# How the last output-projection loads are cut in a fused attention and gated-MLP decode kernel

## The chip, the cores and the metric

The kernel runs on one core of one Trainium2 chip. The metric is the device time of one execution in microseconds, as the median of several runs; the profile is of one further execution, and its span runs from the first to the last recorded instruction.

## The reference

One token `x` (576 values) is normalised and goes through two branches, whose results are added to `x`.

```python
xn = _layernorm(x)
# A: attention over the last W = 4096 keys, 32 query heads on 16 key/value heads of 128
q = (xn @ wq)                       # 576 -> 4096
p = softmax(q k^T * 128 ** -0.5)
o = p v                             # 32 heads x 128 = 4096 values
a = o @ wo                          # 4096 -> 576
# B: gated MLP, 576 -> 2 x 2304 -> 576
z = gelu(xn @ w_in)
b = (z[:2304] * (w_sp * layernorm(z[2304:]) + b_sp)) @ w_out
out = x + a + b
```

All is bf16. The weights and the needed part of the caches come to 51 MB, each byte of which is read once.

## The kernel before

Almost all of the time goes into reading. One engine's queue (SP's) issues every large load, in an order written out by hand, into four large slots of SBUF, tagged `a` to `d`: `wq`, then groups of four heads of K and V (`load_kv`), `w_in` between them, and at the end `w_out` and `wo`. A slot is loaded again as soon as its last reader is done. Each load is one DMA that runs on all 16 DMA engines; on each of these the loads of the queue follow one another. Five small loads (three pieces of `x`, two scalars) come from ScalarE's queue.

The order of work on the other engines is also the order of the program (`manual_schedule`). For each of four groups of heads, VectorE transposes K (`keys`, L264), TensorE makes scores (`scores`, L271), `sm_a` and `sm_b` make the softmax and put the probabilities in place, `pv` multiplies with V (L335), and `tail` normalises (L345, L349), selects (L356) and writes a quarter of the column tile `Y` (`y_copy`, L363). The `w_in` product and the gate lie between the groups and leave their result in `hv`.

The output projection is at the end. `wo` has 4096 rows; they are read as 128 partitions with 32 rows each, so that "row block" t is row t of every partition, 1152 bytes a partition. `Y[:, t, 1]` is the column that belongs to block t. `w_out` has 18 such blocks (`NF`). A block needs four matmuls with two-wide weights (`out_mms`, L471): the 576 columns are cut in four quarters of 144 (`QW`), and two accumulators in PSUM, `acc[0]` and `acc[1]`, take two quarters each, one in each of two rows: the middle column of three holds the values and the other two zeros, so that the choice of `1 - r:3 - r` picks the row. TensorE runs in order: `out_hv` (w_out) around `tail(3)`, then the 32 blocks of wo as they come, then the two copies into `res` (L486, L487) and the store (L488).

The blocks of wo come in five loads (L108, issued at L82), of 14, 9, 6, 2 and 1 blocks. The first two go to the slot of tag `d` (`ends[1]`), the others behind `w_out` in that of tag `a` (`ends[0]`).

The tile framework gives the loads of all queues eight DMA semaphores in turn, in the order of the program as it runs them, and lets a load wait until the load that had its semaphore before has landed. K's second group, whose slot is free from the start, so has a wait for the first piece of `x`.

## Time and profile before

| | |
|---|---|
| median of 3 runs | 126.90 us (126.83 to 126.94) |
| the profiled execution | 126.97 us, span 125.1 us |
| mean granted TensorE clock | 0.754 |
| HBM read | 50.96 MB, 407 GB/s over the span |
| share of the 16 DMA engines' time, SP's queue | 95.3% |
| TensorE matmul busy | 70.2 us (56%) |
| VectorE busy | 78.6 us (63%) |
| ScalarE busy | 43.2 us (34%) |
| GpSimd busy | 7.2 us (6%) |

Times on the page and in the trace count from the start of the span; 1.9 us of the execution lie outside it. A line of the timeline or of a group gives the source line, the engine, the operation and `out<-in` with the tiles' names; the bracket gives idle time of the engine just before and what ended it. `SPq` is SP's sequencer, which issues loads. In the chain of waits, "DMA end<-in_A_wo_dram" is the time from the issue of a wo load to its landing.

### The profile page before, as it was taken

Reading aid. Unit: us, or ns where it says so; the run is one execution under the profiler, and the core shown is the slowest. Engines: PE = TensorE matmul, PEld = TensorE weight load, DVE = VectorE, ACT = ScalarE, POOL = GpSimd, SP = SyncE. Lnnn points to the kernel's source line nnn. Section 1 sums busy time; section 2 is a strip of 40 time slices with the busy share of each in tenths; the row PEclk is TensorE's granted clock in tenths of the full one; section 3 lists DMA queues with packets and bytes.
Section 4 is the critical chain, followed back from the end, with each engine's and each line's share of the span. In section 5 each row is a group of like instructions: output and inputs, shape, how many; then the busy total and the mean of one; then the engine's idle time right before and its main releaser. Section 6 shows DMA issues by size and latency. Waiting matters only on the chain.

```text
span 125.1 us, 1826 instructions
## 1 busy us (share of the span) xinstructions
PE 70.2 (56%) x728; PEld 30.4 (24%) x728; DVE 78.6 (63%) x152; ACT 43.2 (34%) x101; POOL 7.2 (6%) x21
## 2 busy tenths in 40 slices
PE   0012841009886659999580991059892931059972
PEld 0011201001101002999100031002212311026961
DVE  6845135899699976509999367999938359003200
ACT  2100011000000974998079009608701941940000
POOL 2972000000000000000000000000000100000000
PEclk9999997555599958655568599558997555555999
DMA  4999899998999999898999989899998989999960
GB/s 113 507 422 440 363 503 409 430 482 356 498 389 433 385 482 471 377 492 341 492 430 419 471 367 487 359 482 440 409 482 356 492 374 453 414 434 409 413 248 0
DMA packets 2613, 51.06 MB, mean 408 GB/s; under 512 B 300, under 2 KB 430, under 8 KB 686
## 3 DMA queue, kind: packets, MB, share of 16 engines
q1 hardware_dynamic: 2592, 50.96, 95.3%
q8 instruction: 5, 0.08, 0.2%
q14 instruction: 2, 0.02, 0.0%
q10 hardware_dynamic: 14, 0.00, 0.0%
HBM read 50.96 MB, written 0.00 MB: 407 GB/s over the span
## 4 chain that ended last, share of the span: by engine, by line
DMA 62%; DVE 30%; PE 4%; SPq 1%; issue 1%; ACT 0%; DVEq 0%
DMA k<-in_A_k_cache_dram 36%; DMA end<-in_A_wo_dram 25%; DVE kT L264 22%; DVE pt L309 4%; PE S L271 3%; SPq L82 1%; DVE mx L292 1%; DVE on L349 1%; DVE om L345 1%; PE acc L471 0%; PE yps L356 0%; DVE rs L326 0%; ACT res L487 0%; DVE mt L281 0%; DVE mb L287 0%
## 5 line engine op out<-in xcount | busy, mean ns | idle before, releaser
L271 PE MATMUL S<-kT,Qb 128*8 128x512 bf16 x128 | 32.4, 1145 | 23.2 <-DVE kT L264 22.7
L264 DVE STREAM_TRANSPOSE kT<-k 128x1024 f32<-128x1024 f32 x32 | 36.8, 1207 | 6.2 <-DMA k<-in_A_k_cache_dram 6.2
L298 ACT ACTIVATE pz<-S,nm 32x1024 bf16<-32x1024 f32 x16 | 19.2, 1198 | 34.0 <-DVE nm L295 21.1
L312 ACT COPY PT<-pt 32x128 f32<-32x128 f32 x64 | 19.9, 311 | 16.5 <-DVE pt L309 15.8
L335 PE MATMUL ops<-v,PT 128*32 128x512 bf16 x128 | 11.0, 506 | 6.8 <-ACT PT L312 6.8
L271 PEld LDWEIGHTS <-Qb 128*8 128x8 bf16 x128 | 3.6, 96 | 44.9 <-issue 35.4
L309 DVE STREAM_TRANSPOSE pt<-pz 128x1024 f32<-128x1024 f32 x8 | 9.4, 1210 | 0.8 <-ACT pz L298 0.8
L345 DVE SCALAR_TENSOR_TENSOR om<-ops,rs,dmask 128x512 f32<-128x512 f32 x4 | 3.0, 751 | 10.5 <-PE ops L335 10.3
L371 PEld LDWEIGHTS <-win 128*128 128x128 bf16 x126 | 7.9, 166 | 2.0 <-issue 2.0
L371 PE MATMUL zps<-XT,win 128*128 128x2 bf16 x126 | 8.0, 202 | 0.0
L292 DVE TENSOR_REDUCE mx<-S 128x1 f32<-128x1024 f32 x4 | 4.9, 1216 | 4.0 <-PE S L271 3.9
L335 PEld LDWEIGHTS <-PT 128*32 128x32 bf16 x128 | 3.8, 118 | 11.4 <-ACT PT L312 6.9
L229 ACT CAST q_rep<-qps 128x512 bf16<-128x512 f32 x2 | 1.2, 585 | 14.9 <-DVE q_rep L231 14.9
L410 POOL TENSOR_TENSOR mz<-mz,mhalf 128x1 f32<-128x1 f32 x1 | 0.6, 553 | 84.9 <-DVE mz L409 84.9
L186 PE MATMUL ps_x<-ones_b,xtw 1*128 1x1 bf16 x9 | 0.4, 162 | 8.9 <-DVE xtw L184 8.9
L471 PE MATMUL acc<-end,Y 128*2 128x144 bf16 x128 | 4.5, 226 | 0.9 <-DMA end<-in_A_wo_dram 0.8
L231 DVE CAST q_rep<-qps 128x512 bf16<-128x512 f32 x2 | 1.4, 692 | 4.9 <-PE qps L220 4.2
L487 ACT CAST res<-acc 2x144 bf16<-2x144 f32 x1 | 0.3, 270 | 12.0 <-PE acc L471 12.0
L471 PEld LDWEIGHTS <-Y 128*2 128x2 bf16 x128 | 4.1, 84 | 1.2 <-issue 1.2
L356 PE MATMUL yps<-on,sel 128*32 128x32 f32 x32 | 2.0, 210 | 4.1 <-DVE on L349 4.1
L349 DVE TENSOR_REDUCE on<-om 128x128 f32<-128x512 f32 x4 | 4.2, 1043 | 0.1
L486 DVE CAST res<-acc 2x144 bf16<-2x144 f32 x1 | 0.3, 295 | 5.7 <-PE acc L471 5.7
(96 smaller groups left out, 57.6 us busy)
## 6 DMA issues: line engine op xcount, KB each, us to landing
k<-in_A_k_cache_dram SPq DMA_DIRECT2D x4, 4096.0 KB
v<-in_A_v_cache_dram SPq DMA_DIRECT2D x4, 4096.0 KB, 25.4
win<-in_B_w_in_dram SPq DMA_DIRECT2D x1, 4032.0 KB, 26.9
wq<-in_A_wq_dram SPq DMA_DIRECT2D x1, 3584.0 KB, 12.8
end<-in_B_w_out_dram SPq DMA_DIRECT2D x1, 2592.0 KB, 22.3
end<-in_A_wo_dram SPq DMA_DIRECT2D x1, 2016.0 KB
end<-in_A_wo_dram SPq DMA_DIRECT2D x1, 1296.0 KB
rest<-in_B_w_in_dram SPq DMA_DIRECT2D x1, 1152.0 KB
```

The source lines that it names most:

```text
L264: nc.vector.transpose(dst[:, 1024 * n:1024 * (n + 1)], src[:, 1024 * n:1024 * (n + 1)])
L271: nc.tensor.matmul(S[g % 2][32 * x:32 * x + 8, c, :], lhsT=Qb[:, GK * g + x, be].rearrange("p a h -> p (a h)"), rhs=kv[:, be // 2, be % 2, x],
L292: nc.vector.tensor_reduce(out=mx[:, 0:1], in_=s[:], op=ALU.max, axis=mybir.AxisListType.XY)
L298: nc.scalar.activation(pz[lo:hi, :, :, x, :], s[lo:hi].rearrange("p a (t r e) -> p (a t) r e", r=8, e=2), ACT.Exp, bias=nm[lo:hi, 0:1], sc ...
L309: nc.vector.transpose(dst[:, 1024 * n:1024 * (n + 1)], src[:, 1024 * n:1024 * (n + 1)])
L312: nc.scalar.copy(PT4[32 * a:32 * a + 32, :, x, :], pt[32 * x:32 * x + 32, :, 2 * a:2 * a + 2])
L335: nc.tensor.matmul(ops[32 * q:32 * q + 32, :], lhsT=d["PT"][:, t0 // 2:t0 // 2 + 2].rearrange("p t x h e -> p (t x h e)"), rhs=V[g][:, t0: ...
L345: nc.vector.scalar_tensor_tensor(out=om[:].rearrange("p c d -> p (c d)"), in0=ops[:], scalar=d["rs"][:, 0:1], in1=dmask[:].rearrange("p c ...
L349: nc.vector.reduce_sum(on[:], om[:].rearrange("p c d -> p d c"), axis=AXX)
L356: nc.tensor.matmul(yps[32 * g:32 * g + 32, :], lhsT=sel[:, dq, :], rhs=d["on"][:, 32 * dq:32 * dq + 32], start=(dq == 0), stop=(dq == 3), ...
L371: nc.tensor.matmul(zps[:, :, t], lhsT=wt[:, t, :], rhs=XT[:, s, :], start=(s == 0 and t == 0), stop=(s == NS - 1 and t == NF - 1), skip_gr ...
L471: nc.tensor.matmul(acc[n], lhsT=lhs[:, col, 1 - r:3 - r], rhs=wv[:, QW * (2 * r + n):QW * (2 * r + n + 1)], start=False, stop=(last and r ...
```

## The change

The 32 blocks of wo are cut otherwise. Blocks 0 to 25 come in loads of 14 and 12 blocks into the slot of tag `d`, blocks 26 to 28 in one load behind `w_out`. Of block 31, the last 432 columns (864 bytes a partition) come apart from the rest: 128 rows that go into a tile `ext` of their own, 25 rows a load, alternately to partitions 0 to 24 and 80 to 104, two loads to each of `ext`'s three columns of tiles. The three rows left over (125 to 127) are loaded one by one, early, behind the second K group. Block 30 and the first 144 columns of block 31 follow in one load (1440 bytes a partition, they adjoin in memory), and block 29 is the last. That is ten loads for wo at the end instead of five, and three early ones.

Since rows of block 31 now lie in other partitions than the column `Y[:, 31]`, three matmuls with 0/1 weights (`move`, cut from the identity) move that column, and a copy writes it to `Yx`, with a zero where no row lies. `out_ext(j)` does the three quarters of `ext`'s tile j. Tiles 0 and 1 are done before block 26, tile 2 after block 28, then block 30, the first quarter of block 31, and block 29.

All loads from `w_in` on stand lower in the program's text, behind the constants, in the same order of SP's queue; ahead of them come GpSimd's memset of `ext` and the three 1-row loads, which wait for it.

```diff
+XR = 25
+XB = 80
+XN = 3
...
-    win_sb = rows("a", win_h, "win", 0, 7) + rows(rest, win_h, "win", 7, 2, 4096)
-    K[2] = load_kv("b", A_k_cache, 2, "k")
...
-    wo_sb = []
-    for n, t, at in ((14, 1, 0), (9, 1, 14), (6, 0, NF), (2, 0, NF + 6), (1, 0, NF + 8)):
-        wo_sb += rows(ends[t], A_wo, "wo", len(wo_sb), n, at * D)
...
+    ext = const.tile([P, XN, D - QW], BF16, name="ext")
+    nc.gpsimd.memset(ext[:], 0.0)
+    last = A_wo.rearrange("(p s) c -> p s c", p=P)[:, 31, QW:D]
+    for i in range(P - 5 * XR):
+        nc.sync.dma_start(ext[XB + i:XB + i + 1, 2, :], last[5 * XR + i:5 * XR + i + 1])
+    win_sb = rows("a", win_h, "win", 0, 7) + rows(rest, win_h, "win", 7, 2, 4096)
+    K[2] = load_kv("b", A_k_cache, 2, "k")
...
+    for n, t, at in ((14, 1, 0), (12, 1, 14), (3, 0, NF)):
+        wo_sb += rows(ends[t], A_wo, "wo", len(wo_sb), n, at * D)
+    for j in range(5):
+        lo = XB * (j % 2)
+        nc.sync.dma_start(ext[lo:lo + XR, j // 2, :], last[XR * j:XR * j + XR])
+    wo_p = A_wo.rearrange("(p s) c -> p (s c)", p=P)
+    at, w30 = (NF + 3) * D, D + QW
+    nc.sync.dma_start(ends[0][:, at:at + w30], wo_p[:, 30 * D:30 * D + w30])
+    row30 = ends[0][:, at:at + w30]
+    row29 = ends[0][:, at + w30:at + w30 + D]
+    nc.sync.dma_start(row29, wo_p[:, 29 * D:30 * D])
...
+    Yx = const.tile([P, XN, 3], BF16, name="Yx")
+    nc.gpsimd.memset(Yx[:], 0.0)
+    move = const.tile([P, XN, P], BF16, name="move")
+    nc.gpsimd.memset(move[:], 0.0)
+    for j in range(6):
+        lo, n = XB * (j % 2), min(XR, P - XR * j)
+        nc.gpsimd.tensor_copy(move[:, j // 2, lo:lo + n], ident[:, XR * j:XR * j + n])
...
+    yx = ps_m.tile([P, 32], FP32, name="yx", tag="m")
+    for j in range(XN):
+        nc.tensor.matmul(yx[:, j:j + 1], lhsT=move[:, j, :], rhs=Y[:, 31, 1:2], start=True, stop=True)
+    nc.vector.tensor_copy(Yx[:, :, 1], yx[:, 0:XN])
+    def out_ext(j):
+        for q in range(1, 4):
+            out_mm(Yx, j, q, ext[:, j, QW * (q - 1):QW * q])
+
     for t, wv in wo_sb:
-        out_mms(Y, t, wv, t == 31)
+        if t == 26:
+            out_ext(0)
+            out_ext(1)
+        out_mms(Y, t, wv)
+    out_ext(2)
+    out_mms(Y, 30, row30)
+    out_mm(Y, 31, 0, row30[:, D:D + QW])
+    out_mms(Y, 29, row29, True)
```

`out_mm` is the single matmul that `out_mms` was made of; `out_mms` now calls it for the four quarters.

More of the change, by code (lines that the diff above doesn't have):

```diff
@@ L97 @@
     K[1] = load_kv("c", A_k_cache, 1, "k")
-    win_sb = rows("a", win_h, "win", 0, 7) + rows(rest, win_h, "win", 7, 2, 4096)
-    K[2] = load_kv("b", A_k_cache, 2, "k")
-    V[0] = load_kv("c", A_v_cache, 0, "v")
-    K[3] = load_kv("d", A_k_cache, 3, "k")
-    V[1] = load_kv("a", A_v_cache, 1, "v")
-    V[2] = load_kv("b", A_v_cache, 2, "v")
-    V[3] = load_kv("c", A_v_cache, 3, "v")
-    ends = [big.tile([P, TP * DH], BF16, name=f"end{n}", tag="ad"[n]) for n in range(2)]
-    wout_sb = rows(ends[0], B_w_out, "wout", 0, NF, 0)
-    wo_sb = []
-    for n, t, at in ((14, 1, 0), (9, 1, 14), (6, 0, NF), (2, 0, NF + 6), (1, 0, NF + 8)):
-        wo_sb += rows(ends[t], A_wo, "wo", len(wo_sb), n, at * D)
     xrow = const.tile([1, D], BF16, name="xrow")
@@ L179 @@
     nc.gpsimd.memset(mb[:], 0.0)
+    ext = const.tile([P, XN, D - QW], BF16, name="ext")
[5 more added lines that the diff above has]
+    K[2] = load_kv("b", A_k_cache, 2, "k")
+    V[0] = load_kv("c", A_v_cache, 0, "v")
+    K[3] = load_kv("d", A_k_cache, 3, "k")
+    V[1] = load_kv("a", A_v_cache, 1, "v")
+    V[2] = load_kv("b", A_v_cache, 2, "v")
+    V[3] = load_kv("c", A_v_cache, 3, "v")
+    ends = [big.tile([P, TP * DH], BF16, name=f"end{n}", tag="ad"[n]) for n in range(2)]
+    wout_sb = rows(ends[0], B_w_out, "wout", 0, NF, 0)
+    wo_sb = []
+    for n, t, at in ((14, 1, 0), (12, 1, 14), (3, 0, NF)):
[9 more added lines that the diff above has]
+    nc.sync.dma_start(row29, wo_p[:, 29 * D:30 * D])
     xtw = const.tile([1, NS, D // NS, 2], BF16, name="xtw")
@@ L466, with out_mm, out_mms @@
     pv(3)
-    def out_mms(lhs, col, wv, last):
-        for r in range(2):
-            for n in range(2):
-                nc.tensor.matmul(acc[n], lhsT=lhs[:, col, 1 - r:3 - r], rhs=wv[:, QW * (2 * r + n):QW * (2 * r + n + 1)],
-                                 start=False, stop=(last and r == 1), tile_position=(0, 32 * n))
+    def out_mm(lhs, col, q, wv, last=False):
+        n, r = q % 2, q // 2
+        nc.tensor.matmul(acc[n], lhsT=lhs[:, col, 1 - r:3 - r], rhs=wv, start=False, stop=last,
+                         tile_position=(0, 32 * n))
+    def out_mms(lhs, col, wv, last=False):
+        for q in range(4):
+            out_mm(lhs, col, q, wv[:, QW * q:QW * (q + 1)], last and q >= 2)
     def out_hv(c):
         for t, wv in wout_sb[6 * c:6 * c + 6]:
-            out_mms(hv, t, wv, False)
+            out_mms(hv, t, wv)
     out_hv(0)
```

## The prediction

> **What bounds the kernel now.** I read the page first: the slices and the queues.

> ```profile
> PEclk9999997555599958655568599558997555555999
> DMA  4999899998999999898999989899998989999960
> ...
> q1 hardware_dynamic: 2592, 50.96, 95.3%
> q8 instruction: 5, 0.08, 0.2%
> q14 instruction: 2, 0.02, 0.0%
> ```

> The 16 DMA engines are busy from the first slice to the last but one: 51 MB through one queue set the time, and every load waits its turn in it. Seven more transfers are instruction fetches (q8, q14). So I read the end of the chain of waits, and the timeline there:

> ```profile
> 90.70 31.43 DMA end<-in_A_wo_dram
> 122.13 0.04 issue
> 122.17 0.61 PE acc L471 x12
> 122.78 0.02 issue
> ```

> ```profile
> 116.89 0.22 DVE L363 CAST Y<-yps 32x32 bf16<-32x32 f32 x1 [0.53 <-PE yps L356]
> 117.25 2.97 PEld L471 LDWEIGHTS <-Y 128*2 128x2 bf16 x93
> 117.31 3.06 PE L471 MATMUL acc<-end,Y 128*2 128x144 bf16 x92
> 121.14 1.60 PE L471 MATMUL acc<-end,Y 128*2 128x144 bf16 x36 [0.77 <-DMA end<-in_A_wo_dram]
> ```

> The last wo loads were issued at 91 us and land at 121.10 (6 blocks), 122.13 (2) and 122.41 (1). TensorE does four matmuls a block. The first 23 blocks are done by 120.37; it waits for each later load, and after the last landing it needs 0.37 us, to 122.78. The span ends at 125.1; the execution took 126.97, 0.07 over the median of the runs, 126.90.

> The packets in the trace, followed engine by engine, show what the totals hide. All 16 engines get equal shares, but nine finish their last packet at 120.2 to 120.6, two at 120.8 and 121.0, five at 121.7 to 122.0. Each of these seven stood aside once for an instruction fetch: the five 16 KB ones, at 37.4, 57.2, 76.6, 100.7 and 120.1, cost 1.1 to 1.5 us each, which an engine that is never idle doesn't make up. A landing counts when the slowest engine is done, 0.36 us after its last packet, so the five late engines set the end.

> **What the change removes from those engines.** A packet takes 16128 B 0.598, 10368 B 0.386, 6912 B 0.259, 2304 B 0.0895 and 1152 B 0.047 us: 5 ns and 36.7 ns a thousand bytes. By this line 13824 B take 0.513, 3456 B 0.132, 1440 B 0.058 and 864 B 0.037. After the 14-block load an engine now has eight packets each of the 9-, 6-, 2- and 1-block loads: 8 x (0.386 + 0.259 + 0.0895 + 0.047) = 6.25 us. Then it has 12, 3, 1.25 and 1 blocks: 8 x (0.513 + 0.132 + 0.058 + 0.047) = 6.00, so 0.25 less. An engine that serves the 25-row loads gets on top what these carry.

> How many serve them? In every load and store shown the engines used have equal shares: 128 rows on 16, the 2-row store on 2, the 1-row loads on 1. Equal shares of 25 rows are 5 engines with 5 rows, or one with 25. I take 5, the nearer to the loads that use all they can: 25 x 0.037 = 0.92 us, so 0.67 more for each. The five late engines gain 0.25 if they aren't among these, and the nine early ones have 1.1 us to spare. The trace places only one: all five 1-row loads of x and spb run on one and the same engine, which no fetch delayed. So short loads begin at the same engine each time, and I call it engine 0 and take the 25 rows to be on 0 to 4. [...]

> **What it adds to the order of the loads.** The framework deals eight DMA semaphores out in turn, and a load waits until the one eight places earlier has landed: the second K load, with a free slot, has a wait for the first x load's semaphore. With ten loads at the end in place of five, the 1.25-block load waits for the 14-block one (115.93), and the last, block 29, for the 12-block one. Its slowest engine has done the 14 blocks at 115.57; 8 x 0.513 later is 119.68, landed 120.06. SP then issues block 29, behind which nothing is queued. Its packets: the first load of all, 128 rows too, was issued at 0.73 and its engines began at 1.74 to 2.20; so here 121.1 to 121.6. The late engines are busy with 3 + 1.25 blocks until 121.2, the others idle and wait. Eight packets (0.38) and 0.36 to land: 121.85 to 122.3 if they run steadily; 122.9 if they start as cold as the first load's, which lost up to 0.6 more. I take 122.3, since nothing else loads the memory then. [...]

> **What it adds on TensorE.** A matmul of these costs 32 ns (93 weight loads in 2.97), and the last of a row takes 226 ns to its end:

> ```profile
> L471 PE MATMUL acc<-end,Y x128: 222/226/227, 117.3 to 122.5; 128*2 128x144 bf16 x128
> ```

> The 14 blocks (56 matmuls) are done well before 120.06. From there 78 are left: 48 for 12 blocks, 6 for two ext groups, 12 for 3 blocks, 3 ext, 5 for the 1.25 blocks, 4 for block 29. Started at 120.10: the last begins at 120.10 + 77 x 0.032 = 122.56 and ends at 122.79. TensorE reaches block 29 at 122.47, after the landing that I take. So what the late engines gain is not collected: TensorE has been handed twelve blocks at once and becomes the end, 0.01 us from where it was.

> **What lies beside other work.** Three matmuls that move Y's column, with 128-wide weights (L371's of that width take 0.17 + 0.20), come to 0.7 us at most after 117.11, with all wo matmuls queued behind them, and a DVE copy of 0.2, with only the output's copy behind it: TensorE then has 56 x 0.032 = 1.8 us of work and 2.95 until the 12 blocks land. Without that cover they'd cost 0.7. GpSimd:

> ```profile
> 4.83 3.51 POOL L166 MEMSET pz<- 128x4096 bf16 x1
> 8.28 0.12 POOL L176 MEMSET mx<- 128x32 f32 x1
> 8.34 0.12 POOL L179 MEMSET mb<- 128x32 f32 x1
> 11.33 0.55 POOL L203 TENSOR_TENSOR mv<-mv,mhalf 128x1 f32<-128x1 f32 x1 [2.86 <-DVE mv L202]
> ```

> The ext memset, 1296 elements, takes 1296/4096 x 3.51 = 1.1 us from 8.5, inside the 2.86 that GpSimd is idle. The masks for moving (one memset, six copies at 0.14 to 0.2) come after 12 and are next needed at 117; GpSimd's next job is at 97. The moved lines issue nothing new for win, K and V: SP waits for GpSimd's memset (9.6) and issues three 1-row loads by 11, while

> ```profile
> 1.64 1.30 SPq L88 DMA_DIRECT2D k<-in_A_k_cache_dram  x2
> 17.16 0.34 SPq L82 DMA_DIRECT2D win<-in_B_w_in_dram  x1
> ```

> shows it idle between 2.9 and 17.16, waiting for wq; the queue has K1 to carry until 32.8. The ten loads of the end take SP ten issues of 0.43; the first eight have their semaphores 4 us or more before their turn, since the queue is 30 us deep. All of this: nothing.

> **Sum.** 126.90 + 0.01: 126.9, that is, no change. A measurement here tells about 0.2%, 0.25 us.

> **Rivals.** *A fetch-delayed engine is among the five (slower).* It ends the 3 blocks at 120.74, then has 0.92 of 25-row packets, 0.46 and 0.38: 122.54, landing 122.9; TensorE ends 0.36 later, 123.27, so +0.49: 127.4. It decides as soon as one engine's last landing passes 122.47. Against: the x engine is clean. For: five of the other 15 are late. Seven fetches hit seven different engines, so I take them to be dealt in turn; five in a row of 16 that miss engine 0 have 11 places, and 4 of these touch engines 1 to 4: 0.36. Dealt at random, five of 15 miss four given ones in (10 x 9 x 8 x 7) / (15 x 14 x 13 x 12) = 0.15. I hold to the first, and leave it 0.30 for the cases in which the loads begin elsewhere or the fetches fall a little later.

> *Block 29 comes late (slower).* Its wait is new; with the cold start it lands at 122.9: 127.0 to 127.4. For: engines idle by then. [...] 0.08.

> *The change doesn't do what it says (slower).* One engine takes all 25 rows (125 x 0.037 = 4.6 us, end near 129.7), or the loads into one tile wait for each other (five landings, over 130). 0.03.

> *The gain of the queue is collected (faster).* If the late engines go on without a pause they land at 121.59 + 0.36 = 121.95, and 0.36 later is 122.31: -0.47, 126.45. It needs the 78 matmuls in under 2.1 us, 26 ns each. Against: 32 ns in both long rows. Half of it, 126.6, would need 29 ns or 12 blocks that land 0.2 earlier. 0.13.

> *Forecast.* 0.46; its own range is 126.7 to 127.1: 1 ns a matmul is 0.08, and the landing of block 29 may add 0.1.

> So faster 0.13, same 0.46, slower 0.41. The range reaches from half of the gain, 126.55, to the late engine, 127.45; outside lie the whole gain and the failures.

> **What would show it.** Right: the 12 blocks land near 120.1, TensorE runs without a gap from there to 122.8, block 29 lands at 121.9 to 122.45, the 25-row loads by 120.7. Wrong: a gap before the last four matmuls (block 29, or a late engine: then the 25-row loads land after 121.4 as well), matmuls below 30 ns, another clock than the 9s of the last slices, or fetches that fall on other engines or at other times.

## The result and the profile after

| | before | after |
|---|---|---|
| median, runs side by side on one chip | 126.94 us (126.83 to 127.18, 22 runs) | 127.25 us (127.03 to 128.20, 22 runs) |
| ratio | | 1.0032 [1.0021, 1.0042] |
| the same pair, measured again later | 126.81 us | 127.16 us, 1.0028 [1.0014, 1.0041] |

The change makes the kernel slower by 0.3 us, where no change (126.9) had been forecast. That is small, 0.3%, but the interval of the ratio lies wholly above 1, and the repeat agrees. The profiled execution took 128.07 us, but its span is 125.4 us, like that of most runs; the rest lies outside the span, and the last section comes back to it.

The slices and the queues of the page after, against those of before:

```profile
PEclk9999999999997786955558689756999595557999
DMA  4999999998999999999999999999999999999960
...
q1 hardware_dynamic: 2748, 50.96, 95.3%
q8 instruction: 5, 0.08, 0.2%
q14 instruction: 2, 0.02, 0.0%
```

The bytes are the same (50.96 MB), in 156 more packets; the DMA engines are as busy as before; TensorE's granted clock stands at 9 in the last three slices, as before. So neither the queue's amount of work nor the clock tells the two apart. The end of the chain of waits does (start, length, what):

```profile
90.03 30.40 DMA end<-in_A_wo_dram
120.43 0.04 issue
120.47 2.68 PE acc L494 x78
123.15 0.02 issue
123.17 0.27 ACT res L529
```

In before the last link was 12 matmuls behind a load at 122.13. Now it is 78 matmuls in one piece, behind the 12-block load at 120.43. The prediction had exactly this link, with 78 matmuls and 2.69 us (122.79 - 120.10), but started at 120.10. The timeline shows the rest of it:

```profile
117.11 0.23 PE L511 MATMUL yx<-Y,move 128*128 128x1 bf16 x3
117.26 1.92 PE L494 MATMUL acc<-end,Y 128*2 128x144 bf16 x56
120.44 0.35 SPq L198 DMA_DIRECT2D end<-in_A_wo_dram  x1
120.47 1.67 PE L494 MATMUL acc<-end,Y 128*2 128x144 bf16 x48 [1.29 <-DMA end<-in_A_wo_dram]
```

The three column-moving matmuls and the 56 of the 14 blocks are followed by 1.29 us in which TensorE waits for the 12 blocks: they were hidden, as costed. SP issues block 29 0.01 us after the 12 blocks have landed, as its semaphore demands. The DMA view gives issue to landing:

```profile
end<-in_A_wo_dram SPq DMA_DIRECT2D x1, 144.0 KB, 2.2
ext<-in_A_wo_dram SPq DMA_DIRECT2D x5, 21.1 KB
```

Block 29 lands 2.2 us after its issue, at 122.63; TensorE begins its last four matmuls at 123.15 - 0.23 - 3 x 0.032 = 122.82, so that landing is hidden, with 0.2 us to spare.

Landings by the semaphore events in the trace, and the end of TensorE:

| | before | after | before again | after again |
|---|---|---|---|---|
| last packet of the 14 blocks | 115.57 | 115.91 | 115.61 | 115.81 |
| 14 blocks land | 115.93 | 116.23 | 115.98 | 116.23 |
| 12 blocks: last packet, landing | - | 120.02, 120.43 | - | 119.92, 120.59 |
| the five 25-row loads land | - | 120.90 to 121.73 | - | 120.91 to 121.80 |
| last load of wo lands | 122.41 | 122.63 | 122.19 | 122.69 |
| TensorE ends | 122.78 | 123.15 | 122.57 | 123.31 |

### The profile page after: what moved, and what is told of

Same layout as the page of the kernel before. It is cut to its first block, busy times and chain, and to the rows that moved or that the text cites. A ratio compares the mean times of both kernels' runs of the same rounds, so it can differ in the third digit from the quotient of the medians.

```text
span 125.4 us, 1865 instructions
## 1 busy us (share of the span) xinstructions
PE 69.8 (56%) x737; PEld 29.7 (24%) x737; DVE 79.0 (63%) x153; ACT 43.1 (34%) x101; POOL 9.6 (8%) x30
## 3 DMA queue, kind: packets, MB, share of 16 engines
q1 hardware_dynamic: 2748, 50.96, 95.3%
HBM read 50.96 MB, written 0.00 MB: 406 GB/s over the span
## 4 chain that ended last, share of the span: by engine, by line
DMA 61%; DVE 30%; PE 6%; SPq 1%; issue 1%; ACT 0%; DVEq 0%
DMA k<-in_A_k_cache_dram 37%; DMA end<-in_A_wo_dram 24%; DVE kT L288 22%; DVE pt L333 4%; PE S L295 3%; PE acc L494 2%; DVE mx L316 1%; DVE on L373 1%; SPq L85 1%; DVE om L369 1%; PE yps L380 0%; DVE rs L350 0%; ACT res L529 0%; DVE mt L305 0%; DVE mb L311 0%
## 5 line engine op out<-in xcount | busy, mean ns | idle before, releaser
L203 PE MATMUL ps_x<-ones_b,xtw 1*128 1x1 bf16 x9 | 0.4, 163 | 9.1 <-DVE xtw L201 9.1
```

## The experiments

Two theories stood first. **A**: TensorE, handed twelve blocks at once, sets the end. **B**: block 29, which has to wait for the 12 blocks, sets it. Then: the small loads and moved lines cost something by themselves, or the baseline was off. Later came **P** and **Q**, on the 25-row loads. In all versions "before" was run on the same chip; ratios are against that.

**The 12 blocks as 9 and 3.**

```diff
-    for n, t, at in ((14, 1, 0), (12, 1, 14), (3, 0, NF)):
+    for n, t, at in ((14, 1, 0), (9, 1, 14), (3, 1, 23), (3, 0, NF)):
```

> The changed kernel with its load of 12 blocks cut into 9 and 3. Theory A (TensorE is handed twelve blocks at once and ends 78 matmuls of 32 ns after that landing): TensorE has the 9 blocks some 0.8 us earlier and is off the end; from the landing of the 3 blocks only 42 matmuls are left, 1.3 us, so the end passes to block 29, whose issue still waits (for the load of 3 blocks) and which lands 2.2 us after it: 0.1 to 0.2 us under the changed kernel, 127.1. Theory B (block 29's late issue alone sets the end): no change, 127.25. Theory C (the moved lines and early small loads put the whole queue 0.3 us later): still 0.2 to 0.3 over the kernel before in any case.

Measured: 127.05 us, ratio 1.0023 [1.0007, 1.0039]. The chain of waits:

```profile
120.24 2.30 DMA end<-in_A_wo_dram
122.54 0.04 issue
122.59 0.33 PE acc L494 x4
```

With the burst gone, the next bound is B's: the last block, issued at 120.24, lands 2.30 us later, and only its four matmuls follow. TensorE ends at 122.92, 0.23 before the profiled after; 0.1 of this is lost again behind the result, where the span ends 0.93 after the store's landing instead of 0.84 (there are 33 loads and stores now; the run of the small parts below shows this cost alone). Either bound alone is above before's level. A load with a late turn, one whose semaphore comes free only when another load of the end has landed, costs 2.2 to 2.3 us from that landing to its own, and after hides it by 0.2 only because its TensorE is later still.

**A longer burst.**

```diff
-    for n, t, at in ((14, 1, 0), (12, 1, 14), (3, 0, NF)):
+    for n, t, at in ((10, 1, 0), (16, 1, 10), (3, 0, NF)):
```

> The changed kernel with loads of 10, 16 and 3 blocks in place of 14, 12 and 3: the second load ends at the same time and hands TensorE four blocks more. Theory A: 94 matmuls in place of 78 after the landing, 16 x 0.032 = 0.51 us later, 127.75. Theory B: block 29 waits for the same landing, no change, 127.25. Theory C: no change, 127.25.

Measured: 127.71 us, 1.0077 [1.0049, 1.0106].

```profile
120.44 0.04 issue
120.48 3.18 PE acc L494 x94
123.66 0.02 issue
```

The landing is that of after (120.44 against 120.43), with 16 more matmuls behind it: 3.18 - 2.68 = 0.50 us, 31 ns each, and TensorE's end moves by 0.51. That is A shown: this chain sets the end. B alone would have left the end where it was. (Two of this version's six runs are longer outside the span, see the last section; by median span the two versions are 0.4 apart, 125.8 against 125.4.)

**The 25-row loads early, between V2 and V3.** Nothing else changes.

```diff
     V[2] = load_kv("b", A_v_cache, 2, "v")
+    for j in range(5):
+        lo = XB * (j % 2)
+        nc.sync.dma_start(ext[lo:lo + XR, j // 2, :], last[XR * j:XR * j + XR])
     V[3] = load_kv("c", A_v_cache, 3, "v")
```

> The changed kernel with the five loads of 25 rows issued between the third and the fourth V load, so that no load of the end has to wait for a semaphore late; 14, 12, 3, 1.25 and 1 blocks as they were. Theory A: the 12 blocks land as before and 78 matmuls follow, no change, 127.25. Theory B: block 29 lands right behind the 1.25 blocks, near 122.3, and the end comes 0.3 us earlier or more, 126.9 or less. Theory C: as A.

Measured: 127.43 us, 1.0046 [1.0032, 1.0061]; I had expected no change from after.

```profile
120.72 0.04 issue
120.77 2.68 PE acc L494 x78
123.45 0.02 issue
```

No load waits late for a semaphore now, and the same 78 matmuls set the end: B is not needed for it. But the 12 blocks land 0.29 later than in after. The 14 blocks land at 116.60, and the packets say where that comes from: while the 25-row packets ran (93.25 to 95.23), packets of 32768 bytes took 1211 to 1547 ns, median 1317, against 1213 around them. This first hint of a price on other engines' packets is taken up below.

**The small parts alone.** Before's own cut of wo (14, 9, 6, 2, 1), with the moved lines, the memset of `ext`, the three 1-row loads, the masks, and the column-moving matmuls and copy, whose result is not used; what is left out of the change, against after:

```diff
-    for n, t, at in ((14, 1, 0), (12, 1, 14), (3, 0, NF)):
+    for n, t, at in ((14, 1, 0), (9, 1, 14), (6, 0, NF), (2, 0, NF + 6), (1, 0, NF + 8)):
...
-    for j in range(5):
-        lo = XB * (j % 2)
-        nc.sync.dma_start(ext[lo:lo + XR, j // 2, :], last[XR * j:XR * j + XR])
```

> The kernel before with the moved lines, the memset of ext, the three 1-row loads, the masks, and the three matmuls and the copy that move Y's column (their result is not used), but with wo loaded and multiplied as before (14, 9, 6, 2, 1). Theories A and B: the same time as the kernel before, 126.94 within 0.1. Theory C: 0.3 us slower, 127.25, with the 14 blocks landing near 116.2 as in the changed kernel and not 115.9.

Measured: 127.01 us, 1.0015 [1.0006, 1.0024].

```profile
121.23 0.04 issue
121.28 1.39 PE acc L485 x36
122.67 0.02 issue
```

TensorE ends 0.1 after before's repeated run (122.57), on landings 0.09 later; 122.67 is also before's usual end, as worked out below. The 0.2 lies behind the result: the store lands at 124.15 and the span ends 1.07 later, against 0.84 in before, 0.23 more, since SP at the end waits for three more semaphores after the store's (at 124.28, 124.34 and 124.41): with 27 loads and stores instead of 24 the store's semaphore is no longer the last of its order. After has 32, so it doesn't pay this. A version with the loads cut finer, 32 in all, was to get that back:

```diff
-    wout_sb = rows(ends[0], B_w_out, "wout", 0, NF, 0)
+    wout_sb = rows(ends[0], B_w_out, "wout", 0, 9, 0) + rows(ends[0], B_w_out, "wout", 9, 9, 9 * D)
...
-    for n, t, at in ((14, 1, 0), (9, 1, 14), (6, 0, NF), (2, 0, NF + 6), (1, 0, NF + 8)):
+    for n, t, at in ((7, 1, 0), (7, 1, 7), (5, 1, 14), (4, 1, 19), (3, 0, NF), (3, 0, NF + 3), (1, 0, NF + 6), (1, 0, NF + 7), (1, 0, NF + 8)):
```

> The run with the moved lines alone, with five loads cut in two or three (w_out 9 and 9; wo 7, 7, 5, 4, 3, 3, 1, 1, 1), so that there are 32 loads and stores as in the changed kernel, and the store of the output has the last of the eight semaphores again. Theory F (the 0.2 us of the run with the moved lines lie behind the store's landing: SP's closing waits go through the semaphores in order, and three of them, 63 ns each, came after the store's): back to the time of the kernel before, 126.8 on the last chip, within 0.1. Theory C (the early small loads or the moved lines themselves cost 0.2): it stays 0.2 slower.

Measured: 127.16 us, 1.0020 [1.0011, 1.0028]. From the store's landing to the end it is 0.83 again, so that reading holds; but the total missed the expectation:

```profile
113.76 8.81 DMA end<-in_A_wo_dram
122.57 0.04 issue
122.61 0.33 PE acc L485 x4
```

The last landing is now at 122.57, 6.40 after the 14 blocks instead of 6.21 in before's repeat: finer loads run longer (5 + 4 blocks 3.20 us where 9 took 3.10).

**Both kernels again.** Unchanged copies, for the scatter of the landings.

> The kernel before once more, for a second profile of it beside one of the changed kernel. Theory D: the prediction took its end from an execution in which the last landing (122.41) belonged to the engine that the last instruction fetch had just held up, 0.23 us after the other late ones; from the landing of the 14-block load (115.93) to the end it was 6.85 us, where the run with the moved lines has 6.60. So here: 6.6 us, 0.2 to 0.3 less than in the changed kernel. Rival E: the changed kernel's whole queue runs 0.3 us later (its 14 blocks landed at 116.23 in place of 115.93); then here 6.85 again, and the 14 blocks land near 115.9.

> The changed kernel once more. Theory A: 78 matmuls in 2.68 us right behind the landing of the 12 blocks, 4.2 us after that of the 14 blocks, the end 6.92 after it. Theory D: 0.3 us over the kernel before on the same chip, with the 14 blocks landing no later on average. Rival E: the 14 blocks land near 116.2 again.

Measured: before 126.80 us, 1.0001 [0.9991, 1.0011]; after 127.16 us, 1.0028. The chains, before first:

```profile
121.14 0.04 issue
121.18 1.38 PE acc L471 x36
122.57 0.02 issue
```

```profile
120.59 0.04 issue
120.63 2.68 PE acc L494 x78
123.31 0.02 issue
```

Before ends 6.59 us after its 14 blocks here (122.57 - 115.98), where in the profile of the prediction it was 6.85: there the engine with the last instruction fetch (at 120.1) landed 0.23 behind the other late ones. After's profile repeats: the same 78 matmuls, and a 12-block landing even later.

**The burst without anything else.** Before, with only the cut changed: no 25-row loads, no moved lines.

```diff
-    for n, t, at in ((14, 1, 0), (9, 1, 14), (6, 0, NF), (2, 0, NF + 6), (1, 0, NF + 8)):
+    for n, t, at in ((14, 1, 0), (12, 1, 14), (3, 0, NF), (2, 0, NF + 3), (1, 0, NF + 5)):
```

> The kernel before with wo in loads of 14, 12, 3, 2 and 1 blocks, and nothing else of the change: no 25-row loads, no moved lines, no early loads, no load that waits for another at the end. Theory A (TensorE, handed twelve blocks at once, sets the end): the 12 blocks land 4.1 to 4.2 us after the 14, so near 120.15; from there 72 matmuls of 32 ns and 0.2 us: the last ends at 120.15 + 0.08 + 2.30 + 0.2 = 122.7, against 122.57 in the repeated run of before: +0.1 to +0.15, 126.95, and the chain of waits ends with x72 behind the 12-block load. Theory C (the late landings of after come from its own small loads and moved lines): the same chain, but the 12 blocks land 0.2 to 0.4 earlier after the 14 than the 4.20 and 4.36 of after. Rival (the burst has nothing to do with it, the end is the last landing): last landing 122.2, end 122.57, no change.

Measured: 126.83 us, 1.0003 [0.9994, 1.0013].

```profile
120.21 0.04 issue
120.25 2.46 PE acc L471 x72
122.71 0.02 issue
```

The chain has the shape of after's, and yet there is no difference from before. So twelve blocks at once cost nothing measurable when they land at 120.21 with 72 matmuls behind them. After has 78 (0.22 us more: 2.68 - 2.46) and a landing 0.22 to 0.38 later. In this version the 12 blocks' last packet ends at 119.87 and they have landed 0.34 later; in after it ends at 120.02 and the landing takes 0.41, in its repeat 119.92 and 0.67. The 12-block packets took 516 ns in all three. So in after 0.15 of the 0.22 is the later last packet and 0.07 the time from it to the counted landing; in the repeat it is 0.05 and 0.33. That the 25-row loads in flight lengthen this time is not shown: in the version with the early 25-row loads, long done by then, the 12 blocks took 0.45 (120.27 to 120.72), and in before's own profile the two-block load took 0.67 (121.46 to 122.13).

**Versions meant to collect the queue's gain.** All move the 125 rows to the five engines, hand TensorE no more than nine blocks at once, and were meant to have no load with a late turn. First, the five loads joined to two (75 and 50 rows on 25 partitions), behind the 9 blocks:

```diff
+    for n, t, at in ((7, 1, 0), (7, 1, 7), (9, 1, 14), (0, 0, 0), (3, 1, 23), (2, 0, NF), (1, 0, NF + 2)):
...
+            nc.sync.dma_start(ext[0:XR], last[0:3 * XR].rearrange("(j p) c -> p j c", p=XR))
+            nc.sync.dma_start(ext[XB:XB + XR, 0:2], last[3 * XR:5 * XR].rearrange("(j p) c -> p j c", p=XR))
```

> A version meant to collect the gain: the five loads of 25 rows joined to two (75 and 50 rows on 25 partitions), issued behind the 9 blocks; wo in 7, 7, 9, then 3, 2, 1, then 1.25 and 1; the ext matmuls before block 23; 32 loads and stores. Theory A with B: no burst (at most nine blocks and the ext groups, with 1.4 us to spare), and block 29's load waits only for the second 7 blocks, so that the late engines run on: 6.1 us of packets behind the 14 blocks against 6.27 before, the end 6.45 to 6.5 us after that landing; 0.1 to 0.2 us faster than the kernel before, 126.6 to 126.7 on a chip where that takes 126.8. If A and B are wrong (the 25-row packets or the move of Y set the end): 0.3 us slower, like the changed kernel.

Measured: 127.30 us, 1.0034 [1.0022, 1.0046], where 0.1 to 0.2 faster was expected. The last load lands at 122.83, 6.75 after the 14 blocks (116.08), where in before's repeat it is 6.21; the table below gives the packets' part in that. Then the five loads as in after, with wo in 14, 9, (the five), 3, 2, 1, 1.25, 1 and one 3-row load in place of three 1-row loads:

```diff
-    for n, t, at in ((14, 1, 0), (12, 1, 14), (3, 0, NF)):
-        wo_sb += rows(ends[t], A_wo, "wo", len(wo_sb), n, at * D)
-    for j in range(5):
-        lo = XB * (j % 2)
-        nc.sync.dma_start(ext[lo:lo + XR, j // 2, :], last[XR * j:XR * j + XR])
+    for n, t, at in ((14, 1, 0), (9, 1, 14), (0, 0, 0), (3, 1, 23), (2, 0, NF), (1, 0, NF + 2)):
+        if n:
+            wo_sb += rows(ends[t], A_wo, "wo", len(wo_sb), n, at * D)
+        else:
+            for j in range(5):
+                lo = XB * (j % 2)
+                nc.sync.dma_start(ext[lo:lo + XR, j // 2, :], last[XR * j:XR * j + XR])
```

> The changed kernel with its good part kept and its two bad parts taken out: wo in 14, 9, then the five 25-row loads, then 3, 2, 1, 1.25 and 1 blocks; the three rows left over in one load of 3 rows. The last load now waits for a 25-row load that lands by 120, and TensorE never has more than 9 blocks handed at once. Theory A+B (burst and late block 29 ate the queue's gain): the late engines have 0.75 block less, 0.25, and 0.04 for one load more, so the last landing is 0.2 earlier after the 14 blocks than in before (6.0 instead of 6.2) and TensorE ends 0.37 after it: 126.6 to 126.7. Rival (the five engines with the 25 rows, two of them delayed by short fetches, take over as the latest ones, or the small packets slow the others as in the version with two joined loads): the last landing is no earlier than in before, 126.9 to 127.2.

Measured: 127.50 us, 1.0061 [1.0046, 1.0076]. The chain:

```profile
90.72 28.82 DMA end<-in_A_wo_dram
119.54 0.02 issue
119.56 0.33 SPq L85
119.88 0.04 issue
119.93 0.43 SPq L196
120.36 0.04 issue
120.40 2.50 DMA end<-in_A_wo_dram
122.90 0.04 issue
122.94 0.33 PE acc L495 x4
```

The 9 blocks land at 119.54, 3.45 us after the 14 (116.09), where before's take 3.10. My order made this worse: three loads have their turn one after the other behind that landing, at 0.33 to 0.43 us each, and the last, issued at 120.40, needs 2.50. Theory A+B had the late turn right as a mechanism, and I had built it in again; I had expected that load to wait for a 25-row load landed by 120, but SP, in order, was still held by the loads before it.

Then block 31's rows to their own partitions (no column moved, no masks, block 31 as four ordinary matmuls), and the five loads ahead of the 9 blocks, so that nothing has a late turn (the edit of the loads' targets, against the version before this one):

```diff
-                lo = XB * (j % 2)
-                nc.sync.dma_start(ext[lo:lo + XR, j // 2, :], last[XR * j:XR * j + XR])
+                nc.sync.dma_start(ext[XR * j:XR * j + XR], last[XR * j:XR * j + XR])
```

> Block 31's last 432 columns still come in five loads of 25 rows, on the same five engines, but each row goes to its own partition (load j to partitions 25j to 25j+24, the three rows left over in one load), so that block 31 is four ordinary matmuls: no column is moved, no masks, no memset, no ext groups. Order of the loads: 14, the five, 9, 3, 2, 1, 1.25, 1 blocks; the loads that wait for one eight earlier wait for the 14 blocks or a 25-row load, all landed by 118. Theory P (the 25-row packets and the packets of other engines slow each other where they write to the same partitions' part of SBUF): every part of SBUF now gets 25-row packets in turn while the other engines still write there, so packets are still slower than their usual time while the 25-row loads run (10368 bytes over 389 ns, 864 over 40), by 3 to 8 us of engine time in all as in the versions before; last landing no earlier than in before, 126.9 to 127.3. Theory Q (the slowing is due to the 25 narrow partitions 0 to 24 and 80 to 104 that all 25-row loads crowd into): with 128 partitions used the excess falls under 1.5 us, the queue's gain of 0.2 is collected, and the time is 126.6 to 126.7.

Measured: 127.10 us, 1.0032 [1.0020, 1.0044]. And the same with load j taking every fifth row to every fifth partition (`ext[j:5 * XR:5]` from `last[j:5 * XR:5]`):

> As the version with each row to its own partition, but load j takes rows j, j+5, j+10 and so on to partitions j, j+5, j+10: the five engines write in five regions over the whole height of SBUF at any time, and each engine steps five partitions from packet to packet. Theory P: excess as in that version or less, since no engine stays on one part for long; Theory Q: no difference from it; a theory that the memory side is to blame (rows of 864 bytes at a stride of 36864 bytes read by five engines at once): now the stride is five times that, and if that matters the excess changes while the partitions' use hardly does. Time 126.6 to 127.3, within 0.1 of the other by Q.

Measured: 127.09 us, 1.0025 [1.0015, 1.0035]. The chain of the version with rows in their own partitions:

```profile
116.84 0.43 SPq L85
117.28 0.04 issue
117.32 4.93 DMA end<-in_A_wo_dram
122.25 0.04 issue
122.30 0.69 PE acc L486 x12
```

All loads are issued by 118, TensorE has no burst at the end and none of the change's extra matmuls, and still it isn't faster. The packets of the stretch in which the 25-row loads run show why (excess: the sum of what data packets took over their usual time, over all engines, the 25-row packets' own with it):

| version | 25-row packets from, to | what else runs | median ns there, usual | excess, engine us |
|---|---|---|---|---|
| after | 119.02 to 121.02 | 3456 and 1440 bytes, eight 13824 | 135, 135; 516, 516 | 0.6 |
| early, behind V2 | 93.25 to 95.23 | 32768 | 1317, 1211 | 4.7 |
| joined | 117.25 to 119.21 | 10368, 3456, 2304 | 2304: 120, 93 | 5.7 |
| behind the 9 blocks | 117.02 to 119.04 | 10368, 3456, 2304 | 2304: 108, 93 | 3.3 |
| own partitions | 113.90 to 115.91 | 16128, 10368 | 10368: 482, 389 | 4.8 |
| every fifth partition | 114.16 to 115.86 | 16128, 10368 | 10368: 432, 389 | 2.1 |

Where the five loads overlap the full stream, in the last five rows of the table, packets of other sizes slow down, in that stretch and not around it. The rows moved to other engines come back as a tax: by the length of their records the 125 rows of 864 bytes are 125 x 0.040 = 5.0 engine-us of work, and the excess is 2.1 to 5.7. In after itself, where they run in the stream's last microseconds, it is only 0.6 (1.0 in its repeat, 0.1 in the longer burst), so the tax does not account for after's 0.3. With own partitions the 14 blocks, overlapped by the five loads, land at 116.45 instead of before's 115.98: 0.47 later, more than the 0.25 to be gained. Q (the 25 narrow partitions are to blame, and using all 128 brings the excess under 1.5) is refuted by 4.8 and 2.1. P (shared parts of SBUF) foresaw 3 to 8 for own partitions (4.8), and that or less for every fifth (2.1). That the slowing arises on the SBUF side was my guess and is not shown: the wider stride changed what is read as well.

No version beats before.

## Why the prediction came out as it did

**The mechanism held.** TensorE, not a DMA engine, sets the end; 78 matmuls at 32 ns from the 12-block landing; block 29 hidden behind them, landing 2.19 after its issue where 2.24 was taken; the gain of the late engines not collected. The burst took 2.68 us from the start of the first to the end of the last, against 2.69 forecast.

**The term that failed is the landing of the 12 blocks**: 120.06 forecast, 120.43 measured. TensorE's end, forecast at 122.79, came at 123.15, 0.36 later: in this profile that is the whole miss. The prediction had 115.57 for the slowest engine's last packet of the 14 blocks, 8 x 0.513 = 4.10 for the 12, and 0.36 for the landing. Measured:

- The 14 blocks' last packet ended at 115.91, 0.34 later. The prediction took this point over from before as if it were fixed. It is not: the 14 blocks landed at 115.93, 115.98 and 116.09 in three profiles without the early small loads, and at 116.00 to 116.23 in seven with them (those in which no 25-row load runs before that landing). The means are 0.1 apart and each group spreads by 0.2, so how much of the 0.34 belongs to the change stays open. The landings engine by engine give no single cause. In after's first profile twelve engines landed the 14 blocks at 114.17 to 115.22, as in before (114.28 to 115.09), and only the last four, as many as had been held up by a 16 KB fetch by then, came later: 115.93 to 116.23 against 115.70 to 115.93. In the repeats it was the whole queue: the eighth of the 16 landings came at 114.75 in after and at 114.52 in before.
- The 12 blocks took 4.11, as forecast.
- The landing took 0.41, not 0.36 (the sum in fact has 0.38, from 119.68 to 120.06); in the repeat 0.67, while the last packet ended 0.10 earlier than in after's profile. The prediction took one value from before for a time that varies; what lengthens it stays open (see the plain burst). It also had the 25-row loads as pure work for five engines and nothing for the others; the versions above show a price for that, but in after it is small (0.6 engine-us).

So the sum was right as a chain and had no room: the forecast was that TensorE's new end lies 0.01 from the old one, and every delay of that landing goes one for one into the time. The six more matmuls that the change has over the plain burst were in the sum; with the landing at 120.21 of the plain burst, 78 would have ended at 122.93.

**The baseline.** The sum was made against an end at 122.78. Before's repeated run ended at 122.57, for the 0.23 of the last-fetch engine. By the median span of before there, 125.0, and the 2.33 from TensorE's end to the span's end (124.9 - 122.57), 122.67 is the usual end: the old end that the new one was held against was about 0.1 late. In the same way after's repeat, with a median span of 125.3 and 2.29 behind TensorE's end (125.6 - 123.31), has its usual end at 123.0, 0.2 later than the forecast 122.79. Together these are the 0.3 measured; the repeat's profile with its 0.67 was one of the longer executions.

**The 25 rows on five engines.** Each of these loads has five landings (the first one's at 119.61 to 120.90), and the engine of the 1-row x loads is among the five. The prediction took five from the equal shares of before's loads, as an estimate; the trace agrees. An engine began a row every 36 to 37 ns, as forecast (a row's record lasts 40), and the first of the five was through its 25 rows in 0.94 us, with 0.92 forecast. But two of the five are those that the 8 KB fetches had delayed, so that the last row ended at 121.02, and its landing was counted 0.71 later instead of 0.36. So these loads landed by 121.73 rather than 120.7, without setting the end.

**The rivals.** *A fetch-delayed engine among the five*, the heaviest with 0.30 (its sum comes to 122.50, not 122.54), named a slower result, of +0.49, for another reason: none of the five with 16 KB fetches is among them, and no last landing passes TensorE. *Block 29 late*: its mechanism is there, as the version with 9 and 3 shows, but after hides it. The late landing I put at 122.9 for a cold start came at 122.63; its packets did start cold (69 to 375 ns for 1152 bytes instead of 51). *The gain is collected* needed 26 ns a matmul; 31 to 32 it was.

**What was costed at nothing.** The moved lines, the memset (1.18 us, forecast 1.1) and the masks do not show in the chain; TensorE's wait of 1.29 covers the three column matmuls. The small parts alone measured +0.2, which SP's closing waits (0.23) account for; after, with 32 loads and stores, doesn't have these.

## What to carry to other kernels

When a cut of the last loads moves work from late engines to early ones, follow the *consumer* through the new pieces: the time is the last big landing plus all that is queued behind it, and if that sum equals the old end, each small delay upstream shows in full. Price rows given to a few engines not only as those engines' work but by what they do to the others: here 5.0 engine-us of rows brought 2.1 to 5.7 of slower packets where they overlapped the full stream, and 0.6 in after, at the stream's end. Take a baseline from more than one profile when the forecast is a difference of a few tenths, and count the loads in rounds of the semaphores before adding some: a late turn cost 2.2 to 2.5 us, a store that isn't last in its round 0.2.
